# First batch by halves from a table of places; three batches load q once and sum their scores over two 32-row products

## The chip, the cores and the metric

The kernel runs on one NeuronCore of a Trainium2 chip. The metric is the device time of one execution in microseconds (us), median of several runs. PE is the matmul engine (TensorE), PEld its weight loads, DVE VectorE, ACT ScalarE, POOL GpSimd, SP the queue that issues most DMAs. Each engine runs its own instructions in the order in which the program writes them; semaphores tie the engines together.

## The reference

```python
# attention with 32 memory rows: B=8 batches, H=8 heads, S=576, D=64, M=32
a = exp(phi - max(phi, axis=2)); a /= a.sum(axis=2) + 1e-9
k_m, v_m = einsum('bhsm,bhsd->bhmd', a, k), einsum('bhsm,bhsd->bhmd', a, v)
scores = q @ k_m.T / sqrt(64);  attn = softmax(scores);  x = attn @ v_m      # 4608 tokens x 512
# first feed-forward: 512 -> 1536 -> 512
xn = x / sqrt(mean(x*x) + 1e-6) * rms_g
y = (silu(xn @ w_gate) * (xn @ w_val)) @ w_out
# second feed-forward: 512 -> 2048 -> 512
out = relu(y @ w_in)**2 @ w_out2
```

The five weight matrices come as float64, 8 bytes per number, and are turned into float32 on the core.

## The kernel before

**Main loop.** `phase_a` walks over items n = 0, 1, ... An item is one half batch (288 tokens) with one block f of 128 hidden columns: 6 matmuls for the gate (`g`), 6 for the value (`v`), and 12 (`y`) that multiply an earlier item's product with a block of w_out. A batch is 24 items (`NI`). Batch 0 alone takes its items in the order half 0 f 0-5, half 1 f 0-5, half 0 f 6-11, half 1 f 6-11, so that its later weights may come later. ACT takes the Silu of `g` (tile `sl`, L911), DVE multiplies with `v` (L915), ACT and POOL split the product in a high and a low part (`uh` L83, `ul` L92). `g` and `v` have one PSUM bank each, so the next item's gate matmuls wait until ACT has read `g`.

**Attention beside it.** The attention of batch b+1 is computed in steps (`p1`, `p3` to `p7` for the softmax of phi, `t1`, `a2` to `a6` for k_m and v_m, `a7` transposes q, `a8` the scores, `a9` to `a15` their softmax, `a18` to `a23` the mean square and its reciprocal root, `wp_mm` the product of v_m and the gate and value weights, `wp_hi` and `wp_lo` its split). `make_plan` puts each step at one of four places a to d of an item of batch b; `slot` runs them there, in program order, on every engine that the step uses. Batch 0 has no batch before it: `prologue` computes its attention, and also p1 to p6 of batch 1, before item 0.

**Conversions.** The weights are loaded raw by `raw_load` (512 KB each, five buffers) and converted by `conv_next`: two passes on ACT (L139, L140), one on DVE (L148), one on POOL (L152). In order they are the gate and value blocks 0 to 5 (four raws each) with the 12 blocks of w_out between them, 36 raws, then 32 raws of the second feed-forward. A finished gate and value block is 1 MB, goes to DRAM for the other batches (`w1d`, L630), and batch 0 takes it where it lies. `slot` puts three conversions in each of items 0 to 2, two in each of items 3 to 11, then one per item to item 17.

**Loads.** `load_q` brings one pair of heads and needs each row of q twice, at two column offsets (L250), since a 32 by 32 block transpose has to bring both halves of the 64 columns onto one set of 64 partitions: four DMAs of 144 KB per call, 16 per batch. All loads but k and v of batch 0 (ACT's queue) stand in SP's queue.

After the last item of batch 7 come the stages `phase_h` and `phase_z` of the second feed-forward, which the change doesn't touch.

Of the kernel before, what the change touches and what calls it, by code (L numbers as in the profile page):

```python
# [9 lines left out]
F32 = mybir.dt.float32  # L10
# [41 lines left out]
EPS = 1e-9  # L52
RMS_EPS = 1e-6
# [7 lines left out]

class Kernel:
# [41 lines left out]
    def raw_load(self, key):  # L111

        kind, f, cp = key
        nc = self.nc
        t = self.raw.tile([P, DM, 2], U32, tag="raw", bufs=5, name=f"raw_{kind}{f}_{cp}")
# [12 lines left out]
    def convert_start(self, key):  # L128

# [84 lines left out]
    def load_phi(self, b):  # L214
# [3 lines left out]
        for r in range(NR):  # L218
            hs = slice(4 * r, 4 * r + 4)
            nc.sync.dma_start(  # L220
                t[:, hs, 0 : 4 * M], src[r, :, 0:MAIN, :].rearrange("h (p j) m -> p h (j m)", j=4)
            )
            nc.sync.dma_start(t[0:TAIL, hs, 4 * M : 5 * M], src[r, :, MAIN:S, :].rearrange("h p m -> p h m"))
        self.st["ph", b] = t

    def load_kv(self, b, r):
        nc = self.nc
        dma = nc.sync if b else nc.scalar
        t = self.at.tile([P, 2, 4, 5 * D], F32, tag="kv", bufs=2, name=f"kv{b}_{r}")
        for i, src in enumerate((self.k, self.v)):  # L230
            src = src[b].rearrange("(j r) s d -> r j s d", r=NR)[r]
            dma.dma_start(t[:, i, :, 0 : 4 * D], src[:, 0:MAIN, :].rearrange("h (p j) d -> p h (j d)", j=4))
# [3 lines left out]
    def load_q(self, b, c):  # L236
        nc = self.nc

        if b == 0 and c == 2:
            t = self.at.tile([P, M + J * D], F32, tag="L", name="q0_2")  # L240
        elif b == 0 and c == 3:
            t = self.up.tile([P, M + J * D], F32, tag="st", name="q0_3")
        else:
            t = self.at.tile([P, M + J * D], F32, tag="q", bufs=2, name=f"q{b}_{c}")
        for hh in range(2):
            src = self.q[b, 2 * c + hh].rearrange("(p j) d -> p (j d)", j=J)
            for dh in range(2):
                p0 = (2 * hh + dh) * M
                c0 = M * (1 - dh)
                nc.sync.dma_start(t[p0 : p0 + M, c0 : c0 + J * D], src)  # L250
        self.st["q", b, c] = t

# [79 lines left out]
    def t1_first(self, b):  # L332

        t = self.att_ps(f"t1_{b}")
        ex = self.st["ph", b]
        for r in range(NR):
# [10 lines left out]
        self.st["t1"] = t  # L347
# [47 lines left out]
    def a5(self, b):  # L395
        t = self.att_ps(f"kvt_{b}")
        for i in range(2):
# [5 lines left out]
    def a6(self, b):  # L403
# [3 lines left out]
        nc.scalar.activation(kt, t[:, 0:P], AF.Copy)  # L407
# [10 lines left out]
    def a7(self, b, c):  # L418
        q = self.st.pop(("q", b, c))
        qt = self.at.tile([P, S], F32, tag="qt", bufs=4, name=f"qt{b}_{c}")  # L420
        self.nc.vector.transpose(
            qt.rearrange("p (j x) -> p j x", x=M),
            q[:, M : M + J * D].rearrange("p (j d) -> p j d", d=D)[:, :, 0:M],
        )
        self.st["qt", c] = qt

    def a8(self, b, hf):

        ts = [self.att_ps(f"sc_{b}_{hf}_{r}") for r in range(NR)]
        for j in range(4):  # L430
# [19 lines left out]
    def a10(self, b, r, engine="pool"):  # L450
        nc = self.nc
        x = self.st["L"][:, r, :].rearrange("p (j m) -> p j m", m=M)
        lm = self.st["lm"][:, r]
        nc.vector.tensor_reduce(lm, x, axis=AX.X, op=ALU.max)
        (nc.vector if engine == "dve" else nc.gpsimd).tensor_tensor(
            x, x, lm[:, :, None].to_broadcast([P, J, M]), op=ALU.subtract
        )

    def a12(self, b, r):
        x = self.st["L"][:, r]  # L460
        self.nc.scalar.activation(x, x, AF.Exp, scale=1.0 / D**0.5)

    def a13(self, b, r, engine="pool"):
        nc = self.nc
        x = self.st["L"][:, r].rearrange("p (j m) -> p j m", m=M)
        ls = self.at.tile([P, J], F32, tag="ls", bufs=2, name=f"ls{b}_{r}")
# [4 lines left out]
            x, x, ls[:, :, None].to_broadcast([P, J, M]), op=ALU.mult  # L471
        )

    def a15(self, b, r):
        if r == 0:
            self.st["an"] = []
        t = self.at.tile([P, S], F32, tag="qt", bufs=4, name=f"an{b}_{r}")
        self.nc.vector.transpose(t, self.st["L"][:, r, :])
        self.st["an"].append(t)

# [17 lines left out]
    def a19(self, b, hf, cp):  # L498
        at = self.at
        if hf == 0 and cp == 0:  # L500
            self.st["sq"] = [at.tile([P, S], F32, tag="qt", bufs=4, name=f"sq{b}_{i}") for i in range(2)]
            t = at.tile([P, NR, S], F32, tag="L", name=f"sqt{b}")
            self.st["sq"] += [t[:, 0], t[:, 1]]
        for t, sq in zip(self.st.pop("x"), self.st["sq"][2 * cp :]):
            self.nc.scalar.activation(sq[:, hf * HALF : (hf + 1) * HALF], t[:, 0:HALF], AF.Square)

    def sq_add(self, b, hf, engine="pool"):
        eng = self.nc.vector if engine == "dve" else self.nc.gpsimd
        hs = slice(hf * HALF, (hf + 1) * HALF)
        s = [x[:, hs] for x in self.st["sq"]]  # L510
# [3 lines left out]

    def sq_split(self, b, hf):
        t = self.wa.tile([P, NR, HALF], F32R, tag=("anh0", "anl0")[hf], name=f"sqs{b}_{hf}")
        self.split(t[:, 0], t[:, 1], self.st["sq"][0][:, hf * HALF : (hf + 1) * HALF], lo_engine="pool")
# [10 lines left out]
    def a20_first(self, b, hf):  # L528

        t = self.att_ps(f"ss{b}_{hf}")  # L530
        for i, sq in enumerate(self.st["sq"]):
            self.nc.tensor.matmul(
                t[:, 0:HALF], self.ones, sq[:, hf * HALF : (hf + 1) * HALF], start=(i == 0), stop=(i == 3)
            )
        self.st["ss", hf] = t[:, 0:HALF]

    def a21(self, b, hf, part=None):


        nc = self.nc  # L540
        y, a, t = (x[:, hf * HALF : (hf + 1) * HALF] for x in self.st["sq"][1:])
# [14 lines left out]
    def a23(self, b, hf):  # L556
        y = self.st.pop(("ry", hf))
# [18 lines left out]
    def wp_mm(self, b, ch):  # L576
# [12 lines left out]
        self.st["wp"] = ts  # L589
# [7 lines left out]
    def wp_hi(self, b, ch):  # L597
        hi = self.wa.tile([P, NR, DM], F32R, tag=f"wph{ch}", name=f"wph{b}_{ch}")
        for r, t in enumerate(self.st["wp"]):
# [3 lines left out]
    def wp_lo(self, b, ch):  # L603
        lo = self.wa.tile([P, NR, DM], F32R, tag=f"wpl{ch}", name=f"wpl{b}_{ch}")
        for r, t in enumerate(self.st.pop("wp")):
# [12 lines left out]
    def conv_end(self):  # L618
        if not self.started:
            return  # L620
        start = self.started.pop(0)
        kind, f, cp = start[0]
        if kind in "gv":
# [5 lines left out]
            if (kind, cp) == ("v", 1):  # L629
                self.nc.sync.dma_start(self.w1d[f], t.rearrange("p c n -> p (c n)"))  # L630
                self.st["w", 0, f] = t
        else:
# [4 lines left out]
            else:  # L637
                self.nc.sync.dma_start(self.w2d[kind, f], t)
        self.next_raw()

# [9 lines left out]


# [6 lines left out]
    def make_plan(self):  # L658
        self.early, self.warm_ps = 0, None
        self.w1, self.wo, self.wph, self.wpl, self.anh, self.anl = {}, {}, {}, {}, {}, {}  # L660
# [15 lines left out]

        self.plan = {}

        def at(n, pos, step, b, *args):
            if b < B:  # L680
                self.plan.setdefault((n, pos), []).append((step, (b, *args)))


        steps = [
            (1, "a", 0, "a7", 0),
            (1, "a", 0, "load_q", 2),
            (1, "d", 0, "t1"),
# [36 lines left out]
            (16, "c", 0, "sq_add", 0),
            (16, "c", 1, "p7"),
            (17, "b", 0, "a18", 1, 0),
            (17, "c", 0, "a19", 1, 0),
            (17, "d", 0, "a18", 1, 1),
            (17, "d", 0, "a19", 1, 1),
            (18, "a", 0, "sq_split", 0),  # L730
            (18, "c", 0, "sq_add", 1),
            (19, "b", 0, "a20", 0),
            (19, "c", 0, "a21", 0, 0),
            (20, "a", 0, "sq_split", 1),
            (20, "c", 0, "a21", 0, 1),
            (21, "a", 0, "a23", 0),
            (21, "b", 0, "a20", 1),
            (21, "b", 0, "an_split", 0),
            (21, "c", 0, "a21", 1, 0),
            (22, "c", 0, "a21", 1, 1),  # L740
            (23, "c", 0, "a23", 1),
            (24, "d", 0, "an_split", 1),
        ]
        for ch in range(NCH):
            i = 14 + 2 * ch
# [655 lines left out]
```

## Time and profile before

| | |
|---|---|
| median of 3 runs | 1568.76 us (1564.7 to 1569.13) |
| the profiled execution | 1563.32 us, its span 1561.5 us |
| busy in the span | PE 1504.9, DVE 1011.6, ACT 736.9, POOL 666.7 us |
| instructions | 29619 |

The span is the time from the first to the last instruction. An engine's busy time is the sum over its instructions; PE's weight loads run beside its matmuls and are counted apart. "PEclk" is the share of full clock that PE was granted.

### The profile page before, as it was taken

The numbers are of one execution on the slowest core, as the hardware profiler recorded it, in microseconds if no ns is written. First come the engines' busy times: TensorE is split into PE (matmuls) and PEld (weight loads), VectorE is DVE, ScalarE is ACT, GpSimd is POOL, SyncE is SP. The second block draws the span as 40 slices with busy tenths as digits, with TensorE's granted clock in tenths as the row PEclk, the third lists the DMA queues.
The fourth block names the chain that finished last, engine by engine and source line by source line (L and its number), as shares of the span: only waits on it lengthen the run. The fifth ranks groups of instructions, "written<-read, shape, count | busy, mean of one in ns | idle before, by whom it ended". The sixth has DMA issues, their size and how long they took to land. (4 is left out here: it accounts for less than half of the span.)

```text
span 1561.5 us, 29619 instructions
## 1 busy us (share of the span) xinstructions
PE 1504.9 (96%) x11594; PEld 1336.4 (86%) x11594; DVE 1011.6 (65%) x1543; ACT 736.9 (47%) x1318; POOL 666.7 (43%) x657
## 2 busy tenths in 40 slices
PE   6687999999999999999999999999999999999998
PEld 4465798998988889888899888888888999999998
DVE  5755654756456474653675867687667888777774
ACT  2666535445354553534455655566445333333332
POOL 0476634435344453523467521044003654444442
PEclk7788999999999999999999999999999999999999
DMA  9997674565836546432338774455648754444442
GB/s 262 282 310 284 234 203 174 171 169 190 237 137 211 179 160 190 145 99 97 110 139 315 245 263 155 147 162 200 241 170 260 226 147 136 136 125 141 132 132 68
DMA packets 206093, 288.22 MB, mean 185 GB/s; under 512 B 31520, under 2 KB 151328, under 8 KB 197888
## 3 DMA queue, kind: packets, MB, share of 16 engines
q1 hardware_dynamic: 201488, 276.36, 55.2%
q10 hardware_dynamic: 4400, 9.83, 1.8%
q8 instruction: 91, 1.49, 0.4%
q14 instruction: 50, 0.41, 0.1%
q0 software_dynamic: 64, 0.13, 0.0%
HBM read 197.27 MB, written 89.00 MB: 183 GB/s over the span
## 5 line engine op out<-in xcount | busy, mean ns | idle before, releaser
L92 POOL TENSOR_TENSOR ul<-sl,uh 128x288 fp32r<-128x288 f32 x192 | 167.9, 875 | 338.8 <-ACT uh L83 328.2
L881 PE MATMUL y<-uh,woh 128*128 128x288 f32 x768 | 232.5, 303 | 0.0
L882 PE MATMUL y<-uh,wol 128*128 128x288 f32 x768 | 227.6, 296 | 0.0
L883 PE MATMUL y<-ul,woh 128*128 128x288 f32 x768 | 226.8, 295 | 0.0
L83 ACT ACTIVATE S<-sr 128x1792 fp32r<-128x1792 f32 x72 | 122.6, 1703 | 194.7 <-PE z L1323 132.1
L915 DVE TENSOR_TENSOR sl<-sl,v 128x288 f32<-128x288 f32 x192 | 86.0, 448 | 198.3 <-PE v L867 140.8
L92 DVE TENSOR_TENSOR S<-sr,S 128x1792 fp32r<-128x1792 f32 x70 | 143.9, 2056 | 43.3 <-ACT S L83 43.3
L83 ACT ACTIVATE uh<-sl 128x288 fp32r<-128x288 f32 x192 | 85.2, 444 | 170.4 <-DVE sl L915 169.7
L881 PEld LDWEIGHTS y<-uh,woh 128*128 128x128 f32 x768 | 145.1, 189 | 16.0 <-issue 16.0
L882 PEld LDWEIGHTS y<-uh,wol 128*128 128x128 f32 x768 | 145.6, 190 | 0.0
L883 PEld LDWEIGHTS y<-ul,woh 128*128 128x128 f32 x768 | 145.2, 189 | 0.0
L1323 PE MATMUL z<-T,S 128*128 128x256 f32 x504 | 141.3, 280 | 2.1 <-DVE S L92 2.1
L1321 PE MATMUL z<-Wz,S 128*128 128x256 f32 x504 | 141.4, 281 | 0.0
L911 ACT ACTIVATE sl<-g 128x288 f32<-128x288 f32 x192 | 78.3, 408 | 133.4 <-PE g L867 128.0
L1323 PE MATMUL z<-Wz,S 128*128 128x256 f32 x504 | 141.3, 280 | 0.0
L1322 PE MATMUL z<-Wz,S 128*128 128x256 f32 x504 | 141.3, 280 | 0.0
L1321 PE MATMUL z<-T,S 128*128 128x256 f32 x504 | 141.2, 280 | 0.0
L1322 PE MATMUL z<-T,S 128*128 128x256 f32 x504 | 141.2, 280 | 0.0
L1210 ACT ACTIVATE c<-c 128x512 f32<-128x512 f32 (+1 forms) x120 | 70.1, 584 | 136.6 <-DVE c L1236 92.8
L1274 POOL TENSOR_TENSOR sr<-sr 128x256 f32<-128x256 f32 x72 | 98.1, 1363 | 81.8 <-DVE sr L1271 81.8
L865 PE MATMUL g<-anh,wph 128*128 128x288 f32 x384 | 118.4, 308 | 12.6 <-ACT sl L911 10.4
L865 PE MATMUL v<-anh,wph 128*128 128x288 f32 x384 | 119.7, 312 | 3.6 <-DVE sl L915 3.6
(202 smaller groups left out, 4306.4 us busy)
## 6 DMA issues: line engine op xcount, KB each, us to landing
w<-w SPq DMA_DIRECT2D x48, 1024.0 KB, 6.3
sr<-gd SPq DMA_DIRECT2D x144, 256.0 KB, 3.3
gd<-c SPq DMA_DIRECT2D x128, 256.0 KB, 3.0
q<-in_q_dram SPq DMA_DIRECT2D x128, 144.0 KB, 5.1
Wr<-wdi SPq DMA_DIRECT2D x6, 1792.0 KB, 8.9
y<-ys SPq DMA_DIRECT2D x16, 576.0 KB, 3.2
out_dram<-o SPq DMA_DIRECT2D x140, 64.0 KB, 1.7
raw_i<-in_moe_w_in_dram SPq DMA_DIRECT2D x16, 512.0 KB, 4.1
```

The lines of the kernel that those rows point to most:

```text
L83: nc.scalar.activation(hi, src, AF.Copy)
L92: f()
L865: nc.tensor.matmul(out, wh[:, r, cs], ah[:, r], start=(r == 0), stop=False)
L881: nc.tensor.matmul(y, hi[:, cs], uh, start=first, stop=False)
L882: nc.tensor.matmul(y, lo[:, cs], uh, start=False, stop=False)
L883: nc.tensor.matmul(y, hi[:, cs], ul, start=False, stop=last)
L911: nc.scalar.activation(sl, gp, AF.Silu)
L915: nc.vector.tensor_tensor(sl, sl, vp, op=ALU.mult)
L1274: nc.gpsimd.tensor_tensor(t[:, 7], t[:, 2], t[:, 5], op=ALU.subtract)
L1321: nc.tensor.matmul(out, sh, th, start=first, stop=False, **kw)
L1322: nc.tensor.matmul(out, sh, tl, start=False, stop=False, **kw)
L1323: nc.tensor.matmul(out, sl, th, start=False, stop=last, **kw)
```

## The change

`PLAN_0` and `PLAN` are tables of words "step.argument:place", a place being four times the item plus a to d as 0 to 3. `PLAN` holds nearly the places that the attention of batches 2 to 7 had before; `PLAN_0` holds those for batch 1's attention during batch 0, the second half of batch 0's own attention, and each conversion ("conv").

- Batch 0: the prologue takes half 0 (288 tokens) alone through scores, softmax and normalization; half 1 follows in items 0 to 3 (words that begin with 0). p1 to p6 of batch 1 move from the prologue and item 0 to items 2 to 4 (words that begin with 1). The mean square is summed per token into a column (`c20`), the reciprocal root is computed on 96 x 3 numbers (`c21`) and spread over the partitions by three matmuls (`c22`).
- q of batches 0 to 2 (`QS = 3`): `load_qs` brings four heads with one DMA, each row once. The scores are two accumulated products over 32 rows in place of one over 64, and the transpose of k_m goes from PE and ACT to DVE.
- Prologue loads: k on SP's queue, v on ACT's, phi's second half on ACT's; up to eight raws are asked for there (three in buffers that later hold weights). Stores of converted blocks are issued one conversion later. A first Exp and a first Silu on two numbers stand in the prologue; its idle matmuls (`warm`) go from 70 to 46.

```diff
+PLAN_0 = (
+    "0a8.1:0 conv.0:0 0a9.1:1 conv.1:1 conv.2:1 1load_q.0:2 1load_q.1:2 0a10.1:3 0a12.1:3 load_phi:3 "
+    "0a13.1:3 conv.3:4 conv.4:5 0a15.1:6 0wp_mm.1:6 0wp_hi.1:6 0wp_lo.1:6 conv.5:6 0a18.10:6 1load_kv.0:7 "
...
+    def load_qs(self, b, r, hf=None):
...
+        src = self.q[b].rearrange("(i r) (p j) d -> r i p (j d)", r=NR, j=J)[r]
+        nc.sync.dma_start(self.st["q", b, r][:, cs], src[:, :, cs])
...
     def a6(self, b):
...
-        nc.scalar.activation(kt, t[:, 0:P], AF.Copy)
+        if b < QS:
+            nc.vector.transpose(kt, self.st["kvz"][:, 0].rearrange("p r d -> p (r d)"))
+        else:
+            nc.scalar.activation(kt, t[:, 0:P], AF.Copy)
...
     def a8(self, b, hf):
...
+        if b < QS:
+            for r in range(NR):
+                for dh in range(2):
+                    for j in range(4):
+                        rs = slice(j * M, (j + 1) * M)
+                        self.nc.tensor.matmul(
+                            ts[r][rs, 0:HALF],
+                            self.st["kt"][rs, (2 * r + dh) * M : (2 * r + dh + 1) * M],
+                            self.st["qt", 2 * r + dh][rs, hf * HALF : (hf + 1) * HALF],
+                            start=dh == 0,
+                            stop=dh == 1,
+                        )
...
+    def c20(self, b, hf):
...
+        for c in range(NC):
+            cs = slice(c * CH, (c + 1) * CH)
+            for i, sq in enumerate(sqs):
+                self.nc.tensor.matmul(
+                    t[0:CH, 2 * c : 2 * c + 2], sq[:, cs], self.ones[:, 0:2], start=(i == 0), stop=(i == len(sqs) - 1)
+                )
...
     def prologue(self):
...
+        for c in range(KC):
+            self.a7s(0, c // 2, c % 2, 0)
+        h0 = ("h", 0)
+        self.a8(0, 0)
         self.conv_next()
+        self.a9(0, 0)
         self.conv_next()
...
+        self.conv_start()
+        self.a10(0, h0, "dve")
+        self.a12(0, h0)
+        nc.scalar.activation(self.at.tile([P, NR], F32, tag="mc", name="silu_first"), self.ones[:, 0:NR], AF.Silu)
+        self.conv_end()
+        self.a13(0, h0, "dve")
+        self.conv_end()
+        self.conv_start()
+        self.a15(0, h0)
...
+        self.c20(0, 0)
+        self.c21(0, 0)
+        self.c22(0, 0)
         self.wp_lo(0, 0)
         self.a23(0, 0)
         self.an_split(0, 0, "dve")
```

How the change moves instructions is seen at three places. SP's queue, from its start, before (`ph` is phi, `q_0` to `q_3` the four head pairs, `raw` a raw weight):

```order
L220 DMA ph_144<-in_phi_dram 128x4x128
L223 DMA ph_144<-in_phi_dram 64x4x32
L220 DMA ph_144<-in_phi_dram 128x4x128
L223 DMA ph_144<-in_phi_dram 64x4x32
L250 DMA q_0_159<-in_q_dram 32x1152 x4
L250 DMA q_1_164<-in_q_dram 32x1152 x4
L250 DMA q_2_169<-in_q_dram 32x1152 x4
L250 DMA q_3_174<-in_q_dram 32x1152 x4
L220 DMA ph_179<-in_phi_dram 128x4x128
```

and of the change:

```order
L243 DMA ph_145<-in_phi_dram 128x4x128
L244 DMA ph_145<-in_phi_dram 64x4x32
L253 DMA kv_0_150<-in_k_dram 128x4x256
L254 DMA kv_0_150<-in_k_dram 64x4x64
L253 DMA kv_1_155<-in_k_dram 128x4x256
L254 DMA kv_1_155<-in_k_dram 64x4x64
L287 DMA q_0_160<-in_q_dram 128x1x576
L287 DMA q_1_162<-in_q_dram 128x1x576
L836 DMA g_sb<-in_moe_rms_g_dram 128x4x1
L149 DMA raw_g_0_165<-in_moe_w_gate_dram 128x2x512
L149 DMA raw_g_1_167<-in_moe_w_gate_dram 128x2x512
```

Sixteen q loads became two for half 0 (two more follow after six raws), and the first raw moved ahead of them and of batch 1's phi, which stood before all raws. ACT in the prologue, from the softmax of the scores, before (`L` holds the scores, `cv` and `cr` the two passes of a conversion):

```order
L461 ACTIVATE L_390<-L_390 128x576 x2
L139 ACTIVATE cv_g_428<-raw_g_0_184 128x512
L140 ACTIVATE cr_g_429<-raw_g_0_184 128x512
L139 ACTIVATE cv_g_432<-raw_g_1_186 128x512
L140 ACTIVATE cr_g_433<-raw_g_1_186 128x512
L139 ACTIVATE cv_v_448<-raw_v_0_188 128x512
```

and of the change:

```order
L161 ACTIVATE cv_v_386<-raw_v_0_169 128x512
L162 ACTIVATE cr_v_387<-raw_v_0_169 128x512
L161 ACTIVATE cv_v_392<-raw_v_1_171 128x512
L162 ACTIVATE cr_v_393<-raw_v_1_171 128x512
L529 ACTIVATE L_382<-L_382 128x2x288
L870 ACT_TABLE_LOAD
L870 ACTIVATE silu_first<-ones 128x2
L161 ACTIVATE cv_g_411<-raw_g_0_173 128x512
```

Four conversions now stand ahead of the Exp of the scores, which stood ahead of all of them. ACT in items 0 and 1, before, from the first Silu:

```order
L911 ACTIVATE sl_603<-g_587 128x288
L139 ACTIVATE cv_v_612<-raw_v_0_454 128x512
L140 ACTIVATE cr_v_613<-raw_v_0_454 128x512
L83 ACTIVATE uh_621<-sl_603 128x288
L319 ACT_TABLE_LOAD
L319 ACTIVATE ph_179<-ph_179 128x8x128
L319 ACTIVATE ph_179<-ph_179 64x8x32
L139 ACTIVATE cv_v_627<-raw_v_1_469 128x512
L140 ACTIVATE cr_v_628<-raw_v_1_469 128x512
```

and of the change, from the split of item 0's product:

```order
L109 ACTIVATE uh_573<-sl_545 128x288
L529 ACT_TABLE_LOAD
L529 ACTIVATE L_382<-L_382 128x2x288
L161 ACTIVATE cv_o_600<-raw_o_0_430 128x512
L162 ACTIVATE cr_o_601<-raw_o_0_430 128x512
L947 ACT_TABLE_LOAD
```

The Exp of batch 1's phi has left this place (it stands in item 4), and the Exp of half 1's scores has come to it.

## Rows read from the trace of the kernel before

**Rows 1.** The page's 40 slices of the span: PE busy, granted clock, DMA.

```profile
PE   6687999999999999999999999999999999999998
PEclk7788999999999999999999999999999999999999
DMA  9997674565836546432338774455648754444442
```

**Rows 2.** Busy time in stretches: prologue, items 0-2, 3-5, 6-12, 13-23, batches 1, 2.

```profile
core 0: us, PE busy (x) PEld busy (x) DVE busy (x) ACT busy (x) POOL busy (x), PEclk, DMA share, GB/s
0.00:52.40 52.40, 35.67 (x341) 21.08 (x341) 30.12 (x59) 14.36 (x30) 5.98 (x11) 0.74 0.98 260
52.40:75.90 23.50, 14.74 (x224) 11.04 (x224) 16.83 (x28) 17.52 (x30) 12.15 (x10) 0.78 0.89 301
75.90:97.70 21.80, 16.50 (x108) 11.73 (x106) 11.72 (x20) 14.03 (x28) 17.25 (x16) 0.84 0.91 289
97.70:142.00 44.30, 33.56 (x235) 27.12 (x235) 22.09 (x38) 30.17 (x55) 30.78 (x26) 0.92 0.91 309
142.00:198.20 56.20, 51.85 (x385) 39.10 (x386) 39.32 (x67) 30.51 (x68) 34.40 (x34) 0.91 0.62 230
198.20:293.00 94.80, 94.44 (x833) 83.20 (x833) 55.24 (x101) 43.75 (x95) 42.36 (x46) 1.00 0.58 186
293.00:387.90 94.90, 94.57 (x835) 83.36 (x834) 54.45 (x98) 44.55 (x97) 42.42 (x47) 1.00 0.59 186
```

**Rows 3.** Who waited for whom, 30 to 160 us, longest in total first.

```profile
PE g L865 <- ACT sl L911: 10.4, 6, 3.2
...
ACT woh L83 <- POOL cv_o L152: 8.9, 4, 3.9
...
PE wp L582 <- DVE sqt L543: 8.0, 2, 7.7
...
ACT cv_o L139 <- DMA raw_o<-in_moe_w_out_dram: 3.6, 1, 3.6
```

**Rows 4.** Timeline of the prologue, one engine at a time: ACT, DVE, PE.

```profile
11.52 1.28 ACT L319 ACT_TABLE_LOAD   x1 [11.52 <-DMA kv<-in_v_dram]
...
11.22 0.27 DVE L313 TENSOR_TENSOR ph<-ph,mx 64x128 f32<-64x128 f32 x1
...
20.03 0.42 DVE L390 TENSOR_TENSOR kvz<-kv,rs 128x256 f32<-128x256 f32 x1 [0.26 <-PE kv L377]
...
24.96 0.78 DVE L421 STREAM_TRANSPOSE qt<-q 128x576 f32<-128x576 f32 x1 [1.85 <-DMA q<-in_q_dram]
...
28.73 0.71 DVE L454 TENSOR_REDUCE lm<-L 128x18 f32<-128x576 f32 x1
...
39.69 0.78 DVE L478 STREAM_TRANSPOSE an<-L 128x576 f32<-128x576 f32 x1
...
46.10 0.45 DVE L543 TENSOR_SCALAR sqt<-ss 128x288 f32<-128x288 f32 x1
...
49.82 0.46 DVE L553 SCALAR_TENSOR_TENSOR sq<-sqt,sq 128x288 f32<-128x288 f32 x1
...
42.24 2.29 PE L532 MATMUL ss<-sq,ones 128*128 128x288 f32 x4 [0.46 <-ACT sq L505]
...
52.37 0.40 PE L865 MATMUL g<-anh,wph 128*128 128x288 f32 x1 [2.00 <-ACT anh L83]
```

**Rows 5.** Timeline rows for single costs: small DVE operations, 40 small matmuls, one conversion.

```profile
15.33 0.17 DVE L364 RECIPROCAL rs<-rs 128x2 f32<-128x2 f32 x1
...
13.49 1.58 PE L340 MATMUL t<-ones,ph 128*32 128x2 f32 x80 [1.28 <-ACT ph L319]
...
60.62 0.66 ACT L140 ACTIVATE cr_v<-raw_v 128x512 int32<-128x512 uint32 x1
```

**Rows 6.** Timeline of PE: scores of one half of batch 1 (16 records, eight matmuls).

```profile
99.50 0.71 PE L433 MATMUL sc<-qt,kt 64*32 64x288 f32 x16
```

**Rows 7.** Timeline of SP's queue: the issue of batch 0's q.

```profile
3.42 17.83 SPq L250 DMA_DIRECT2D q<-in_q_dram  x16
```

More of the change, by code (lines that the diff above doesn't have):

```diff
@@ L114, in raw_load @@
         nc = self.nc
-        t = self.raw.tile([P, DM, 2], U32, tag="raw", bufs=5, name=f"raw_{kind}{f}_{cp}")
+        pool, tag, bufs = (self.wa, self.raw_more.pop(0), 1) if self.raw_more and len(self.raws) >= 5 else (self.raw, "raw", 5)
+        t = pool.tile([P, DM, 2], U32, tag=tag, bufs=bufs, name=f"raw_{kind}{f}_{cp}")
         src = {"g": self.w_gate, "v": self.w_val, "i": self.w_in2, "o": self.w_out1, "z": self.w_out2}[kind]
@@ L330, in p7, with t1_first @@
         nc.vector.tensor_tensor(es[0:TAIL, hs], es[0:TAIL, hs], ex[0:TAIL, hs, 4 * M : 5 * M], op=ALU.add)
-    def t1_first(self, b):
-        t = self.att_ps(f"t1_{b}")
+    def t1_first(self, b, r=None):
+        if not r:
+            self.st["t1"] = self.att_ps(f"t1_{b}")
+        t = self.st["t1"]
         ex = self.st["ph", b]
-        for r in range(NR):
+        for r in range(NR) if r is None else (r,):
             for jt in range(5):
@@ L396, in a5 @@
         t = self.att_ps(f"kvt_{b}")
-        for i in range(2):
+        for i in range(b < QS, 2):
             self.nc.tensor.transpose(
@@ L470, in a13, with a15 @@
         (nc.vector if engine == "dve" else nc.gpsimd).tensor_tensor(
-            x, x, ls[:, :, None].to_broadcast([P, J, M]), op=ALU.mult
+            x, x, ls[:, :, :, None].to_broadcast(list(x.shape)), op=ALU.mult
         )
[L474 to L479, printed above, removed]
+    def a15(self, b, part):
+        kind, i = part
+        if i == 0:
+            self.st["an"] = [None, None]
+        for r in (i,) if kind == "r" else range(NR):
+            if i == 0 or kind == "r":
+                pool, tag, bufs = (self.at, "qt", 4) if b else (self.wa, ("wph5", "wpl5")[r], 1)
+                self.st["an"][r] = pool.tile([P, S], F32, tag=tag, bufs=bufs, name=f"an{b}_{r}")
+            hs = slice(0, S) if kind == "r" else slice(i * HALF, (i + 1) * HALF)
+            self.nc.vector.transpose(self.st["an"][r][:, hs], self.st["L"][:, r, hs])
     def a18(self, b, hf, cp):
@@ L526, in a20 @@
         self.st["ss", hf] = t[:, 0:HALF]
[L528 to L535, printed above, removed]
     def a21(self, b, hf, part=None):
         nc = self.nc
-        y, a, t = (x[:, hf * HALF : (hf + 1) * HALF] for x in self.st["sq"][1:])
+        y, a, t = self.st["sq", hf][1:]
         if part != 1:
@@ L620, in conv_end @@
             return
-        start = self.started.pop(0)
+        start, n = self.started.pop(0), len(self.stores)
         kind, f, cp = start[0]
@@ L637, in conv_end @@
             else:
-                self.nc.sync.dma_start(self.w2d[kind, f], t)
+                self.stores.append((self.w2d[kind, f], t))
         self.next_raw()
+        old, self.stores = (self.stores, []) if not self.conv_keys else (self.stores[:n], self.stores[n:])
+        for to, t in old:
+            self.nc.sync.dma_start(to, t)
     def wo_split(self):
@@ L659, in make_plan @@
         self.early, self.warm_ps = 0, None
+        self.raw_more = ["wph3", "wpl3", "wpl4"]
+        self.stores = []
         self.w1, self.wo, self.wph, self.wpl, self.anh, self.anl = {}, {}, {}, {}, {}, {}
@@ L744, in make_plan @@
-        for ch in range(NCH):
-            i = 14 + 2 * ch
-            steps += [(i - 3, "d", 0, "wst_load", ch), (i, "a", 0, "wp_mm", ch), (i, "b", 0, "wp_ev", ch)]
-        at(1, "c", "a21", 0, 1, 0)
-        at(2, "a", "a23", 0, 1)
-        at(2, "d", "an_split", 0, 1)
-        for b in range(B - 1):
-            for i, pos, ahead, step, *args in steps:
-                if (b, step) == (0, "t1"):
-                    step = "t1_first"
-                at(NI * b + i, pos, step, b + 1 + ahead, *args)
@@ L756, in make_plan, with steps @@
-        at(0, "c", "p6", 1)
-        for n, ch in ((1, 1), (3, 2), (7, 3), (10, 4), (13, 5)):
-            at(n, "c", "wp_mm_early" if n == 1 else "wp_mm", 0, ch)
-            at(n, "c", "wp_hi", 0, ch)
-            at(n, "c" if n == 1 else "d", "wp_lo", 0, ch)
-        at(1, "c", "a21", 0, 1, 1)
+        def steps(text, b):
+            name, _, x = text.partition(".")
+            if name == "conv":
+                return [("conv_next", ())]
+            x = [int(c) for c in x]
+            if name[0].isdigit():
+                b, name = int(name[0]), name[1:]
+            elif name in ("p1", "p3", "p4", "p5", "p6", "p7", "load_phi", "load_kv") or name == "load_q" and x[0] < 2:
+                b += 1
+            if b < QS and name in ("load_q", "a7"):
+                if name == "load_q" and x[0] >= 2:
+                    return []
+                name, x = name + "s", x if name == "load_q" else [x[0] // 2, x[0] % 2]
+            if name in ("a10", "a12", "a13", "a15"):
+                x = [("r" if b else "h", x[0])]
+            if name in ("a10", "a13") and not b:
+                x.append("dve")
+            if name == "t1" and b == 1:
+                name = "t1_first"
+            if name == "wp_mm" and (b, x) == (0, [1]):
+                name = "wp_mm_early"
+            return [(n, (b, *x)) for n in (("a18", "a19") if name == "a18" else (name,)) if b < B]
@@ L764, in slot @@
+        self.plan = {}
+        for b in range(B - 1):
+            for word in (PLAN if b else PLAN_0).split():
+                text, _, q = word.partition(":")
+                self.plan.setdefault((NI * b + int(q) // 4, int(q) % 4), []).extend(steps(text, b + 1))
     def slot(self, n, pos):
-        for step, args in self.plan.get((n, pos), ()):
+        for step, args in self.plan.get((n, "abcd".index(pos)), ()):
             getattr(self, step)(*args)
@@ L785, in prologue @@
         nc = self.nc
-        nc.scalar.dma_start(self.g_sb, self.rms_g.rearrange("(c p) -> p c", p=P))
+        nc.scalar.activation(self.at.tile([P, NR], F32, tag="rs", name="exp_first"), self.ones[:, 0:NR], AF.Exp)
         self.load_phi(0)
@@ L789, in prologue @@
         self.load_kv(0, 1)
-        for c in range(KC):
-            self.load_q(0, c)
+        for r in range(NR):
+            self.load_qs(0, r, 0)
+        nc.sync.dma_start(self.g_sb, self.rms_g.rearrange("(c p) -> p c", p=P))
+        self.next_raw(6)
+        for r in range(NR):
+            self.load_qs(0, r, 1)
+        self.next_raw(8)
         self.load_phi(1)
-        self.next_raw()
         self.warm(30)
```

261 lines of the change are left out of this document (112 added, 149 removed), and 23 rows, old and new, of tables (PLAN, PLAN_0).

## The prediction

> **What bounds the kernel now.** I read the page's slices first: PE is at 9 tenths in all slices from the fifth on, and below that in the first four, about 156 us [rows 1]. So whatever can be won lies there, and everything that adds PE work later costs its full price. The stretches confirm it: batches 1 and 2 take 94.8 and 94.9 us with PE busy 94.4 and 94.6 of them, at a granted clock of 1.00 [rows 2]. Ahead of them lie a prologue of 52.4 us, in which no main matmul runs, and batch 0, which takes 23.5 + 21.8 + 44.3 + 56.2 = 145.8 us for the same 24 items, with five more weight products: 51 us more than a dense batch. That is what the change works on.
>
> What fills batch 0? PE is idle for 8.8 + 5.3 + 10.7 + 4.4 = 29 us of it and runs partly at the lower of its clock levels (mean 0.78 to 0.92, between half and full, which are 1.2 and 2.4 GHz) [rows 2]. PE's own waits there end with a Silu on ACT (10.4 us) and with the reciprocal root on DVE (7.7 in one piece) [rows 3]. ACT is busy 17.5 of 23.5 us in items 0 to 2, and a good deal of that is conversions, which stand in its order ahead of the next Silu. DMA is at 0.89 to 0.98 of its time until 142 us [rows 2], but a conversion waited for its raw only once, 3.6 us [rows 3]. So DMA is full yet mostly hidden; the chain of ACT, DVE and POOL in program order is what PE waits for.
>
> In the prologue the chain can be followed: a table load for the Exp from 11.52 to 12.80, the last q transpose waiting for its DMA until 24.96, softmax from 28.73 to the last transpose's end at 40.47, squares, their sum, the reciprocal root from 46.10 to 50.28, the first main matmul at 52.37 [rows 4].
>
> **The change, part by part.**
>
> *Prologue up to the softmax.* phi is ready for its Exp at 11.49, and the table load then stands in the way [rows 4]; the new first Exp loads the table beside the first DMAs, so 1.3 us go. SP needed 17.83 us to issue batch 0's sixteen q loads [rows 7]; now two DMAs carry half of the tokens and each row once, 0.59 MB in place of 2.36. k_m and v_m then set the time, not q. From them (about 18.7, that is the 20.03 at which their scaling began [rows 4], less 1.3) I count their scaling and transposes 1.3, four half transposes of q 4 x 0.41 (half of the 0.78 row) = 1.6, scores about 3.5 at the low clock, their transposes 0.5: softmax starts at 25.7, not 28.7: **-3.0**.
>
> *Softmax of one half.* One pass over 576 columns in place of two: half of the 11.74 from 28.73 to 40.47 [rows 4], 5.9. Both orders have conversion steps between them on DVE; the new one has one or two more per pass, 0.8, and its Exp stands behind four conversions on ACT, for which I add 1.0. 7.7 in place of 11.74: **-4.0**. This cover is thin: four conversions are 4 x 1.3 us of ACT [rows 5], and they need raws 0 to 3 landed by about 24 us. By bytes, 5.6 MB at 260 GB/s [rows 2] are there at 22.
>
> *Mean square.* Before, 42.24 (first sum) to 50.28 [rows 4]. Now 12 two-column matmuls; 40 others took 1.58 us [rows 5], these load three times as many columns of weights, so 0.5 to 2, I take 1.2; nine operations on 96 x 3 numbers at 0.17 (the smallest DVE row, [rows 5]) 1.5; three small matmuls 0.5; hand-overs 0.8. 4.0 in place of 8.0: **-4.0**. The second half's q transposes (1.6 on DVE) lie beside the squares; if q's second half, which stands behind six raws in SP's queue, lands after 34 us, they are late and the reciprocal root with them.
>
> First main matmul: 52.4 - 11.0 = about **41.4**.
>
> *Batch 0's items.* What left the prologue comes back here. Half 1 brings to ACT an Exp, four squares and one table load more: 576 and 4 x 288 columns at the pace of 0.66 for 512 [rows 5] and 1.28 [rows 4], 3.5. To DVE it brings a softmax pass of about 5 and score transposes of 0.9, less the 2.7 by which the root is shorter, and p1 to p5 of batch 1 two passes over 1024 columns, about 3 at the pace of 0.71 for 576 [rows 4]: 6.2. Part of it hides in engines that are 54 to 75% busy there [rows 2]; I take 5.0 as the loss in items 0 to 5 (bounds 3.5 and 9.7, the one engine alone and both in a row). Against it, the 7.7 us wait for the root (nine operations of half a batch behind conversions on DVE) becomes a wait for nine short ones, behind which the y matmuls and the next gate still stand in PE's order: I take 3.0 of it as won (0 to 5). In items 6 to 12, 44.3 us for seven items at 309 GB/s, 2.36 MB fewer have to be loaded by then (1.18 each for batches 0 and 1), 7.6 us of DMA time, of which the one seen wait is 3.6; I take 4.0 (0 to 8). In items 13 to 23 batch 2's 1.18 MB and the later conversions give 2.0 (0 to 5). Sum: 5 - 3 - 4 - 2 = **-4.0**.
>
> *Scores over 32 rows.* The eight matmuls of one half, over 64 rows each, took 0.71 us together [rows 6], so they ran at the same time. Now sixteen, of which four can run beside each other (row block j writes column block j) and the four groups follow each other; that is between one more group (0.7) and four times the row (2.8) for a half, I take 2.1, so +1.4. In batches 0 and 1 that lies where PE waits anyway; batch 2's two halves lie in the dense stretch: **+2.9**, less one transpose of k_m, 0.3. *Loads of q in fewer DMAs* free SP's queue, which is not waited for; the later stores of converted blocks and the 24 fewer idle matmuls, which run while PE waits, I cost at nothing: the first are read back half a batch later, the second only keep the clock up, and PE is not what the first items wait for.
>
> Sum: -11.0 - 4.0 + 2.6 = -12.4, and 1563.3 - 12.4 = 1550.9 for an execution like the profiled one. The runs shown lie 1.4 to 5.8 above that execution (median 5.4); I add 1.4 and forecast **1552 us**.
>
> **A shape that could turn the DMA saving around.** The new q load has four heads as the slowest dimension of its source, [4, 32, 576]; no load of the kernel before has fewer than 32 there. If a load is spread over no more DMA engines than that dimension has entries, q's 1.18 MB go through 4 engines of 16. At 309 GB/s and a share of 0.91 [rows 2] one engine moves 21 GB/s, so a batch's q keeps those four busy for 14.0 us, where the old double load kept all sixteen busy for 7.0, and every later load waits for its part on those four: +7 us of DMA time for each of three batches in place of -3.5.
> The Trainium skill (DMA: Bandwidth & Descriptors, the section on why a DMA increments its semaphore by 16) states such a rule: the number of engines is the largest up to 16 that divides the slowest dimension on both sides. No row here shows a load to which it would apply; by it the sum would be that of rival 2.
>
> **Rivals.**
> 1. *The loads were the true limit, and all of the saving is real*: DMA is at 0.9 until 142 us, which speaks for it; that raws were waited for once only speaks against it. The bounds of the items' terms then hold: 3.5 - 5 - 8 - 5 = -14.5 in place of -4, so about **1541**.
> 2. *q on four DMA engines*, as above. Two batches' q fall before 142 us, 14 us of DMA time; the slack there is a tenth of 90 us, so some 6 hide and 8 remain, and the 4.0 of items 6 to 12 turns to nothing as well, partly inside the same 8: 1552 + 8 = **1560**.
> 3. *The head start is given back*: batch 0 ends when its 36 conversions and their ACT, DVE and POOL steps are through (ACT and POOL 30 us in 44 in items 6 to 12 [rows 2]), whenever it began. Then 7 to 11 of the 11 us go: **1562 to 1566**, no change that can be measured.
> 4. *Slower: conversions block the Silu.* In the new order SP brings k, v, phi and q of batches 1 and 2 between the raws, and ACT's Silu stands behind the conversions. Fourteen conversions lie in items 2 to 8; if each waits 1 us or more for its raw, 14 us of PE waits eat the whole gain, from 17 us on the kernel is slower by over 0.3%; at 2 us each it is 12.4 - 28 = 15.6 worse, **1580**. Against it: eight raws are under way at the start, not five.
>
> **Chances and range.** The forecast 0.42 (its own range 1547 to 1557), rival 1 0.20, rival 2 0.20, rival 3 0.11, rival 4 0.07. About 0.3%, 4.7 us, is what a measurement of this kernel can tell from no change, so faster means below 1564. Faster: 0.42 + 0.20 + most of rival 2 (0.17) + 0.02 = 0.81; same 0.12; slower 0.07. The range takes in rivals 1 and 2 and the near end of rival 3: 1538 to 1565.
>
> **What the profile after would show.** First gate matmul at 39 to 44 us; Exp of phi with no table load before it; the root as nine DVE rows under 0.25 us. Item 6 at 85 to 92 (before 97.7), batch 1's first item at 181 to 186 (before 198.2), and batch 1's 24 items, which hold batch 2's scores, at about 97.4. ACT waiting on DMA for a raw after 45 us would speak for rivals 2 or 4; q's loads landing over 6 us apart for rival 2; a first matmul at 41 but batch 1 at 195 for rival 3. The prediction is wrong if half 0's chain waits for raws in the prologue, or if batches 3 to 7 are not the same as before.

## The result: slower, 1578.0 us in place of 1568.0

The changed kernel takes 1578.03 us (median of 4 runs, 1577.12 to 1579.29), the kernel before on the same chip 1567.97: a ratio of 1.0068 (95% interval 1.005 to 1.0086). The forecast was 1552 with a range to 1565. The profiled execution's span is 1575.5 us, 14.0 more than before.

Busy time in stretches of the changed kernel, with the edges of [rows 2] (prologue, items 0-1, 2-5, 6-12, 13-23, batches 1 and 2; the second edge lies an item earlier, at item 2):

```profile
0.00:48.60 48.60, 28.83 (x307) 18.35 (x307) 21.02 (x53) 14.10 (x27) 7.24 (x12) 0.65 0.85 249
48.60:69.50 20.90, 12.43 (x88) 6.47 (x88) 11.27 (x23) 15.95 (x30) 12.62 (x11) 0.74 0.54 185
69.50:98.60 29.10, 26.22 (x311) 23.40 (x309) 17.85 (x34) 19.96 (x38) 19.67 (x19) 0.83 0.95 301
98.60:143.60 45.00, 36.38 (x282) 30.00 (x282) 24.83 (x40) 23.83 (x50) 27.36 (x24) 0.89 0.98 290
143.60:207.80 64.20, 52.47 (x385) 40.61 (x386) 36.47 (x67) 38.23 (x76) 33.91 (x34) 0.87 0.64 230
207.80:305.40 97.60, 97.24 (x865) 84.64 (x864) 55.14 (x102) 43.61 (x94) 42.50 (x47) 1.00 0.53 168
305.40:400.30 94.90, 94.52 (x834) 83.33 (x833) 54.28 (x98) 44.55 (x97) 42.38 (x46) 1.00 0.59 186
```

The prologue is 3.8 us shorter than before [rows 2], not 11; items 0 to 12 take 95.0 us (before 89.6) and items 13 to 23 take 64.2 (before 56.2), so batch 1 begins at 207.8, 9.6 later than before. Batch 1 then costs 2.8 more, batch 2 nothing. In items 0 and 1 the DMA engines are busy for 0.54 of the time where they had been at 0.9, though loads were wanted. Finer stretches of the same kernel show it plainly, each with the share next to last:

```profile
40.00:50.00 10.00, 7.08 (x42) 6.40 (x35) 4.62 (x16) 2.91 (x6) 0.00 (x0) 0.50 0.98 369
50.00:60.00 10.00, 8.16 (x70) 4.17 (x68) 4.58 (x11) 7.38 (x14) 5.16 (x4) 0.90 0.35 120
60.00:70.00 10.00, 3.44 (x18) 1.66 (x19) 5.53 (x11) 7.68 (x16) 7.95 (x7) 0.61 0.70 241
```
```profile
53.00:60.00 7.00, 5.16 (x42) 2.75 (x34) 4.01 (x10) 4.38 (x8) 3.89 (x3) 1.00 0.25 97
157.00:159.00 2.00, 2.00 (x18) 0.83 (x4) 0.00 (x0) 1.97 (x4) 1.51 (x2) 0.50 0.26 104
```

The DMA share is the mean over 16 engines. From 53 to 60 us, behind batch 1's q, it stays at 0.25, which is four engines of sixteen; some time behind batch 2's q it is at that level again (0.26 from 157 to 159 us). SP's queue has the reason just ahead of the first stretch: batch 1's two loads of q, and behind them loads of phi of which one stood at issue for 9.15 us, where the two ahead of it took 1.2 and 2.2.

```profile
44.54 2.73 SPq L287 DMA_DIRECT2D q<-in_q_dram  x2
47.36 2.19 SPq L243 DMA_DIRECT2D ph<-in_phi_dram  x1
49.61 1.19 SPq L244 DMA_DIRECT2D ph<-in_phi_dram  x1
50.85 9.15 SPq L243 DMA_DIRECT2D ph<-in_phi_dram  x1
```

Batch 2's two loads of q are issued at 119.9 and 122.0. Twenty us later ACT waits for raws (first two rows), its Silu (third) stands behind those conversions, and PE's next gate (last row) waits 7 us for the Silu:

```profile
142.04 0.66 ACT L161 ACTIVATE cv_o<-raw_o 128x512 f32<-128x512 f32 x1 [6.90 <-DMA raw_o<-in_moe_w_out_dram]
...
149.88 0.66 ACT L161 ACTIVATE cv_o<-raw_o 128x512 f32<-128x512 f32 x1 [3.31 <-DMA raw_o<-in_moe_w_out_dram]
...
153.00 0.41 ACT L947 ACTIVATE sl<-g 128x288 f32<-128x288 f32 x1
...
153.46 0.61 PE L901 MATMUL g<-anh,wph 128*128 128x288 f32 x1 [6.98 <-ACT sl L947]
```

Before, the one wait for a raw in that part was 3.6 us [rows 3]; the forecast had named such waits after 45 us as the sign of rivals 2 and 4. From batch 2's first item (305.42, before 293.04) to the last item of batch 7 (856.32, before 842.35) another 1.6 us are lost. Of these 1.1 lie between the first and the last item of batch 7 (77.99 us, before 76.92), a stretch that the change doesn't touch and that takes from 76.9 to 81.7 us in the profiled executions of this text; batches 3 to 6 are each within 0.5 us of before.

In the prologue the last loads of k and v are late for PE (first two rows), the scores and the 24 records of `c20` run at the lower level (0.50, 1.2 GHz), and the root's nine operations take 0.16 us each, as forecast; the last row but one waits for them:

```profile
21.33 1.94 PE L414 MATMUL kv<-kv,ph 128*32 128x128 f32 x32 [4.53 <-DMA kv<-in_v_dram]
23.64 0.65 PE L414 MATMUL kv<-kv,ph 64*32 64x128 f32 x8 [0.38 <-DMA kv<-in_v_dram]
...
26.15 4.06 PE L485 MATMUL sc<-qt,kt 32*32 32x288 f32 x32 [0.84 <-DVE qt L472]
...
40.18 0.48 PE L596 MATMUL ss<-ones,sq_0h 128*96 128x2 f32 x2
...
46.08 1.57 PE L622 MATMUL rb<-ident,ryc 96*128 96x96 f32 x6 [1.90 <-DVE ryc L614]
48.67 0.61 PE L901 MATMUL g<-anh,wph 128*128 128x288 f32 x1 [1.02 <-ACT anh L109]
```

### The profile page after: what moved, and what is told of

Same layout as the page of the kernel before. It is cut to its first block, busy times and chain, and to the rows that moved or that the text cites. A ratio compares the mean times of both kernels' runs of the same rounds, so it can differ in the third digit from the quotient of the medians.

```text
span 1575.5 us, 29778 instructions
## 1 busy us (share of the span) xinstructions
PE 1512.3 (96%) x11707; PEld 1347.1 (86%) x11707; DVE 1000.9 (64%) x1552; ACT 741.4 (47%) x1321; POOL 661.8 (42%) x657
## 4 chain that ended last, share of the span: by engine, by line
PE 83%; DVE 5%; ACT 4%; DMA 4%; issue 2%; POOL 2%; SPq 0%; POOLq 0%; DVEq 0%; ACTq 0%
PE z L1357 7%; PE z L1359 7%; PE z L1358 7%; PE y L917 5%; PE y L919 5%; PE y L918 5%; PE h_S L1134 4%; PE h_S L1135 4%; PE h_S L1136 4%; PE v L901 3%; PE h_A L1134 3%; PE h_A L1135 3%; PE h_A L1136 3%; PE g L901 3%; PE v L902 3%; PE v L903 3%
## 5 line engine op out<-in xcount | busy, mean ns | idle before, releaser
L1310 POOL TENSOR_TENSOR sr<-sr 128x256 f32<-128x256 f32 x72 | 92.8, 1289 | 83.4 <-DVE sr L1307 83.4
```

## Experiments

Two questions: is it the shape of the q load (rival 2), and why does batch 0 not keep the head start? All are compared with the kernel before, which took 1566.9 to 1568.4 in these comparisons.

**1. The same load, one DMA per head** (32 source rows each, in all q loads of batches 0 to 2):

```diff
-        nc.sync.dma_start(self.st["q", b, r][:, cs], src[:, :, cs])
+        for i in range(4):
+            nc.sync.dma_start(self.st["q", b, r][i * M : (i + 1) * M, cs], src[i, :, cs])
```

> The changed kernel with its new q load cut into one DMA per head (32 rows each, the same bytes, four times as many DMAs). Theory 'few engines' (a q load whose source has four heads as its slowest dimension runs on a quarter of the DMA engines): the stretch in which the changed kernel had a DMA share of 0.54 (48.6 to 69.5 us) goes back to about 0.9, and the time falls from 1578 to 1555 to 1565 us. Theory 'order' (the loss comes from the new order of conversions and Silus on ACT, whatever the loads' shape): within 3 us of 1578.

Measured 1560.09, ratio 0.9965 (0.995 to 0.998): the same bytes in more DMAs are 18 us faster, and the change turns from a loss into a small gain. Its stretches (prologue, items 0-1, 2-5, 6-12, 13-23, batch 1):

```profile
0.00:41.20 41.20, 26.20 (x307) 16.40 (x307) 21.04 (x53) 14.00 (x27) 7.28 (x12) 0.80 0.86 248
41.20:62.20 21.00, 12.50 (x88) 6.54 (x88) 11.27 (x23) 15.87 (x30) 12.56 (x10) 0.74 1.02 319
62.20:91.00 28.80, 26.55 (x311) 23.72 (x309) 17.25 (x34) 19.86 (x38) 19.69 (x19) 0.83 0.88 271
91.00:134.50 43.50, 36.54 (x282) 30.30 (x283) 26.07 (x43) 27.27 (x54) 27.64 (x25) 0.88 1.01 316
134.50:191.30 56.80, 50.52 (x386) 39.11 (x385) 35.45 (x64) 34.75 (x72) 33.68 (x34) 0.91 0.67 248
191.30:288.90 97.60, 97.23 (x865) 84.63 (x864) 55.15 (x102) 43.58 (x94) 42.52 (x46) 1.00 0.53 168
```

The first main matmul is at 41.29, items 0 and 1 have a DMA share of 1.02 in place of 0.54, and no wait for a raw is left past the prologue. Items 13 to 23 are back at 56.8.

**2. Two heads per DMA** (slowest dimension 2):

```diff
+        for i in range(0, 4, 2):
+            nc.sync.dma_start(self.st["q", b, r][i * M : (i + 2) * M, cs], src[i : i + 2, :, cs])
```

> The changed kernel with its new q load cut into two DMAs of two heads each (the same bytes). 'Few engines': the slowest dimension is two now, each load takes twice as long as in the changed kernel, so 28 us per batch, and the time rises by 15 to 45 us. 'Order', or a cost that lies in the size of the loads: no change, within 3 us of 1578.

Measured 1603.97, ratio 1.0242 (1.0217 to 1.0266): more DMAs than in the change, and 26 us slower than it. The stretch that held 0.35 now holds 0.18, and in the middle of it the share stays at 0.13, two engines of sixteen:

```profile
60.00:70.00 10.00, 5.48 (x42) 3.34 (x39) 7.82 (x15) 6.00 (x9) 5.23 (x4) 0.84 0.18 67
70.00:80.00 10.00, 6.06 (x31) 4.25 (x30) 3.24 (x5) 7.01 (x15) 8.62 (x7) 0.50 0.23 75
62.00:71.00 9.00, 4.48 (x34) 1.99 (x33) 6.46 (x12) 7.00 (x11) 5.22 (x5) 0.82 0.13 50
```

With slowest dimensions of 2, 4 and 32, 1604, 1578 and 1560 us: neither bytes nor the number of DMAs sets the cost, the shape does. The rule of the Trainium skill (DMA: Bandwidth & Descriptors, the section on why a DMA increments its semaphore by 16) gives 2, 4 and 16 engines for them. The traces agree: 0.13 and 0.25 of sixteen engines are 2.1 and 4.0, and with 32 the share is 1.02; no view counts the engines of one DMA by itself.

**3. Loading once, undone** (`QS = 1`: batches 1 and 2 load q twice and score over 64 rows, as before), without and with the head-by-head load for what is left:

> The changed kernel with the new q load and the 32-row scores for batch 0 alone (QS = 1); batches 1 and 2 load q twice, as before. 'Few engines': two of the three slow loads are gone, 7 us of DMA time each, and the 2.8 us of longer scores in batch 1's items; 1561 to 1569 us. 'Order': 2.8 us less alone, about 1575 us.

> Both edits: QS = 1, and batch 0's q with one DMA per head. 'Few engines': below QS = 1 alone by the one remaining slow load, 1555 to 1562 us; against the first kernel of this set it shows whether loading q of batches 1 and 2 once is worth its 2.8 us of scores (if DMA binds, up to 7 us slower than the first; if not, up to 3 us faster). 'Order': about 1575 us.

Measured 1564.82 (ratio 0.9982, 0.9967 to 0.9998) and 1559.44 (0.995, 0.9935 to 0.9965). With the first, the first main matmul stays late (48.47) but batch 1 starts at 197.15 in place of 207.80; with the second they are at 41.78 and 191.76. Batch 0's own four loads so cost 5.4 us, those of batches 1 and 2 the rest, some 13 (experiment 4 has 4.0 and 13.9). Against experiment 1 the second starts batch 1 at the same time (191.76 and 191.30) with 2.36 MB more to load, though without batch 1's 32-row scores in batch 0. So fewer bytes are worth no more there than those scores cost, some 3 us by the row at the end of this text, and not 7.6; and batch 1's items are 2.7 us shorter (94.9) without batch 2's.

**4. Only the loads of batches 1 and 2 as in the change**, batch 0's by head:

```diff
+        if b:
+            nc.sync.dma_start(self.st["q", b, r][:, cs], src[:, :, cs])
+        for i in () if b else range(4):
```

> The changed kernel with batch 0's four q loads (two halves of two rows) made head by head, and those of batches 1 and 2 left as one DMA of four heads each. All by head took 1560.1 us, all in one DMA 1578.0; first main matmul at 41.29 and 48.67, batch 1's first item at 191.30 and 207.80. Theory 'few engines, everywhere' (each DMA of four heads holds back the loads behind it by its own length): first main matmul at 41 to 42, items 0 to 12 within 3 us of the run by head, and the loss of about 10 us comes in items 13 to 23, where batch 2's q is loaded: 1568 to 1572. Theory 'prologue' (only the loads at the start matter, for later ones are hidden): 1559 to 1562. Theory 'head start given back' (batch 0 ends when the slowest load and conversion are through, so a loss at the start is no loss at the end): 1576 to 1579.

Measured 1574.02 (7 runs, 1568.47 to 1577.47), ratio 1.0036 (1.0017 to 1.0054). The first theory (1568 to 1572) and the third (1576 to 1579) both miss by 2 us, 'prologue' (1559 to 1562) by 12. 'Prologue' falls. The place is nearly that of the first: items 13 to 23 take 67.4 us, 10.6 more than by head. But item 13 begins at 140.0 (134.5 by head, where the theory allowed 3 us) and the first main matmul at 43.9. Of these last 2.6 us 1.5 are there when k_m is transposed (19.30 against 17.84), where the two kernels have run the same program: so much do executions differ in the prologue.

In the profiled execution the lead over the change shrinks from 4.8 us at the first main matmul to 3.6 at item 13, 2.0 at item 15 and 0.4 at batch 1 (207.4): ACT waits 10.2 us for `raw_o` between 120 and 166 us, as in the change, and PE 8.5 us for the Silu. That is the third theory's picture, but this execution was the slowest of the seven (1577.47), and the median lies 4.0 below the change's. How much of a lead at the start reaches the end is therefore not shown.

**5. The first items in another order.** With the loads mended, 150.0 us of batch 0's items are still 8 above the forecast's 141.8 and 4 above before. PE's waits from 41 to 191 us in experiment 1 have changed their kind: the Silu (10.4 before [rows 3]) has 1.5 left and the root is nearly gone, but half 1's products now make PE wait:

```profile
PE x L561 <- DVE an L552: 4.0, 1, 4.0
PE x L561 <- ACT sq L581: 3.9, 1, 3.9
PE sc L486 <- DVE wpl L712: 3.9, 1, 3.9
PE x L561 <- DVE wpl L712: 3.5, 1, 3.5
PE mx_None L333 <- DVE wpl L712: 2.3, 1, 2.3
PE rb L623 <- DVE ryc L615: 1.9, 1, 1.9
PE g L902 <- ACT sl L948: 1.5, 3, 0.8
```

On top of the second kernel of experiment 3 the words of `PLAN_0` were moved, and nothing else; then also batch 1's scores:

```diff
-0a13.1:3 conv.3:4 conv.4:5 0a15.1:6 0wp_mm.1:6 0wp_hi.1:6 0wp_lo.1:6 conv.5:6 0a18.10:6 ... 0a18.11:7 ... 0c20.1:9
+0a13.1:3 conv.3:4 0wp_mm.1:5 0wp_hi.1:5 conv.4:5 0wp_lo.1:6 0a15.1:6 conv.5:6 0a18.10:7 ... 0a18.11:9 ... 0c20.1:11
...
-a8.0:31 a9.0:32 ... a8.1:32 a9.1:34 ... p3:35 ... p4:44 ... p5:45
+a8.0:35 a9.0:36 ... a8.1:37 a9.1:38 ... p3:36 ... p4:46 ... p5:47
```

> The kernel with q loaded head by head and 32-row scores for batch 0 alone (1559.4 us, span 1555.1), with the steps of half 1 placed otherwise in items 1 to 3: the second chunk's weight product and its conversion to two parts one place earlier (ahead of a conversion on ACT), the two products of half 1 (x) one and two places later, so that the second stands behind item 2's gate, and its mean square two places later. No work is added or left out. There item 2's gate began at 62.70, behind waits of 4.0 and 3.9 us for x, while the second chunk's low part could be ready near 57. Theory 'order' (the head start of 11 us was lost because PE, in program order, waits in items 1 and 2 for half 1's softmax and squares): those two waits go, item 2's gate starts at 56 to 59, and 3 to 6 us of it reach batch 1's first item (now 191.8) and the end: 1553 to 1557. Theory 'conversions' (batch 0 ends when its 36 conversions are through, however it began): item 2 begins earlier, but batch 1's first item stays within 1 us of 191.8 and the time at 1558 to 1561. Theory 'work' (the PE time of half 1, 9.4 us, was moved out of the prologue and is what fills the items): no wait is worth much, 1557 to 1560.

> The same, and in items 7 to 11 batch 1's scores placed one item later (behind item 8's gate, value and output products instead of ahead of them) and its largest-value product half an item later. There PE waited 4.3 us at 103.7 and 2.3 us for the low part of a weight product (on DVE), since the scores' PSUM banks are those of that product. Theory 'order': both waits go, item 13 starts 5 to 7 us earlier than in the run with the first items alone and at least 4 of it reach batch 1: 1549 to 1553. Theory 'conversions': item 13 moves by under 2 us and the time stays within 2 us of that run. Theory 'work': as 'conversions' to within 2 us.

Measured 1555.65 (0.9921, 0.9907 to 0.9935) and 1555.39 (0.9925, 0.9912 to 0.9939). The first has the numbers of 'order': item 2's gate at 58.63 in place of 62.70, batch 1 at 188.33 in place of 191.76, the time 3.8 less. 'Work' (1557 to 1560) misses, and 'conversions' falls for these items: most of what is won in item 2 is there 130 us later. Yet of the two waits only the one for the squares went; the other grew from 4.0 to 5.3:

```profile
PE x L561 <- DVE an L552: 5.3, 1, 5.3
```

The second is a miss of 'order': one of its two waits went, the other shrank from 2.3 to 1.6, and others came (3.0 us for score transposes, 5.7 in all for the Silu in place of 3.1, and 4.7 us on ACT for a raw in place of 0.7). Item 13 began 1.4 us earlier (128.68), batch 1 at 188.94, and nothing is won: for this edit 'conversions' and 'work' had it right.

**6. Half 1's products behind item 2's gate, the second chunk's split earlier still**, and the same with batch 1's q loaded once (`QS = 2`):

```diff
-0a13.1:3 conv.3:4 0wp_mm.1:5 0wp_hi.1:5 conv.4:5 0wp_lo.1:6 ... 0a18.10:7 ... 0a18.11:9 ... 0c20.1:11 ... 0c22.1:12
+0a13.1:3 0wp_mm.1:4 0wp_hi.1:4 0wp_lo.1:4 conv.3:4 conv.4:5 ... 0a18.10:9 ... 0a18.11:11 ... 0c20.1:12 ... 0c22.1:13
```

> The run with the first items placed otherwise, and more of it: the second chunk's conversion to two parts straight behind half 1's Exp on ACT (there it stood behind one conversion, a table load and the Silu), and both products of half 1 (x) behind item 2's gate and value products. In that run PE waited 5.3 us for x's operand ahead of item 2's gate at 58.63 and the low part of the second chunk was ready at 56.7. Theory 'order': item 2's gate starts at 55 to 57, and what is won (2 to 3.5 us) is still there at batch 1 (now 188.33): 1552 to 1554. Theory 'conversions' (batch 0 ends when its conversions are through): batch 1 stays at 188 to 189, 1555 to 1556.

> As the run with x behind item 2's gate, and batch 1's q too loaded once (head by head) with its scores as two sums over 32 rows: 1.18 MB less to load in batch 0, and some 3 us more of PE time for the scores in items 7 to 9. Theory 'order' (PE and the chain of its operands set the time in batch 0): 1 to 3 us slower than that run. Theory 'DMA' (the loads set the time until about 142 us): 2 to 4 us faster than it.

Measured 1559.14 (0.9949, 0.993 to 0.9968) and 1561.26 (0.9956, 0.9941 to 0.9971). Both theories missed the first: item 2's gate came at 57.29, little earlier, and then the squares that free the banks for the second product stood on ACT behind three conversions and a Silu (timeline of ACT from the last of the three, then PE):

```profile
65.99 0.65 ACT L161 ACTIVATE cv_v<-raw_v 128x512 f32<-128x512 f32 x1
66.84 0.67 ACT L162 ACTIVATE cr_v<-raw_v 128x512 int32<-128x512 uint32 x1 [0.20 <-POOL w L174]
67.42 0.40 ACT L948 ACTIVATE sl<-g 128x288 f32<-128x288 f32 x1
67.71 0.71 ACT L581 ACTIVATE sq<-x 128x288 f32<-128x288 f32 x2
...
68.17 1.52 PE L561 MATMUL x<-an,kvz 32*64 32x288 f32 x8 [5.11 <-ACT sq L581]
```

Batch 1 started 9.0 later than in the first kernel of experiment 5 (197.34). The profiled execution was the slowest of its six (1563.28); by the medians the loss is 3.5 us. It is the direction that 'order' gives for a new wait of 5.1 us ahead of item 3's gate; the placing was worse. Between the two kernels of this pair the intervals overlap, so the last pair of theories stays undecided.

## Why the prediction was wrong, step by step

**The step that failed first: "q on four DMA engines ... some 6 hide and 8 remain".** The mechanism was named and given 0.20; its price was 18 us (1578 against 1560), not 8, so the forecast stood on the wrong case and rival 2's own time was as wrong. Two errors are in the price. It counted two batches' q, those of batches 0 and 1, while batch 2's is issued before 142 us too (119.9 and 122.0); and it put batch 0's at no time in the prologue, where the first main matmul came 7.4 us later (48.67 against 41.29). Nearly all of that was lost ahead of the scores, for k_m was late, in the change (first row) against experiment 1 (second):

```profile
24.82 0.31 DVE L445 STREAM_TRANSPOSE kt<-kvz 128x128 f32<-128x128 f32 x1
```
```profile
17.84 0.31 DVE L446 STREAM_TRANSPOSE kt<-kvz 128x128 f32<-128x128 f32 x1
```

And it took the DMA engines' average slack as cover (a tenth of 90 us, that is 9, of which it let 6 hide). Here four loaded engines were not covered by idle time of the other twelve (share 0.25 from 53 to 60 us): raws queued behind landed late, the conversion that waited stood ahead of a Silu on ACT, and PE stopped. That is rival 4's chain, set off by rival 2's cause. I had priced them apart.

**Prologue, -11.0 to 41.4: the total right where the load doesn't interfere** (41.29 in experiment 1), **in part by luck.** There the softmax began at 24.0 (forecast 25.7) and took 7.5 us (forecast 7.7). The mean square, with the three matmuls behind the root, took 5.7 us (34.60 to 40.27; forecast 4.0). The one error pays for the other. `c20`'s twelve matmuls were mis-sized: forecast 1.2 us, 2.2 at full clock in experiment 1 (first row) and 4.0 at the lower level in the changed kernel (second). The three matmuls took 1.57 us, forecast 0.5.

```profile
34.60:36.80 2.20, 2.20 (x32) 2.11 (x24) 0.00 (x0) 1.09 (x2) 0.00 (x0) 0.99 1.11 357
```
```profile
40.10:44.10 4.00, 4.00 (x32) 3.91 (x24) 0.00 (x0) 1.08 (x2) 0.00 (x0) 0.50 0.99 376
```

**Batch 0's items, -4.0: wrong by 8 even with the loads mended** (150.0 against 141.8). The term costed half 1's work on ACT and DVE, never on PE. PE is busy 126 us in experiment 1's items (the sum of its four rows) and 117 before [rows 2]. That the prologue's PE time fell by the same 9.5 us (35.7 to 26.2) is chance, for 3.3 of it are the idle matmuls left out (before, then experiment 1):

```profile
L782 PE MATMUL warm<-ones 128*128 128x256 bf16 x70 | 13.1, 372 | 1.4 <-DVE ones L172 1.4
```
```profile
L827 PE MATMUL warm<-ones 128*128 128x256 bf16 x46 | 9.7, 401 | 1.4 <-DVE ones L194 1.4
```

By line, the items' products for x take 7.0 us in place of 3.2, the scores 8.9 in place of 1.4 (half 1's, and batch 1's over 32 rows), and half 1's mean square and its spread 3.7; the weight products take 13.9 in place of 21.4. In items 0 to 5, 2.5 us more were lost than forecast, and experiment 5's first kernel, set beside the kernel it was made from (49.7), gives 2.1 back by placing alone (47.5, forecast 47.3). In items 6 to 12 that kernel comes near the forecast 40.3 (40.9), but with half of the bytes that the forecast wanted saved (batch 1's) still loaded, so its reason isn't borne out. Items 13 to 23 stay at 56 to 60 in place of 54.2 in every kernel with mended loads. They take 56.4 and 56.8 us where batch 1's q is loaded once (`QS` 2 and 3) and 58.2 to 60.3 where it is loaded twice, and of these kernels only the latter let ACT wait for a raw past the prologue (0.7 to 4.7 us in all). The first kernel of experiment 3, which reaches item 13 late (142.3) and loads it twice, takes 54.8. So the loads may set the time there; no run separates it.

**32-row scores: right.** Batch 1 took 97.6 for 97.4. PE's records by line over that batch have 4.3 us for its scores, where two halves took 1.4 [rows 6]:

```profile
L485 PE MATMUL sc<-qt,kt 32*32 32x288 f32 x64 | 4.3, 404 | 0.0
```

**Rival 1** (all DMA saving real, 1541) falls with experiments 1 and 3. **Rival 3** (head start given back) holds in part: of 11.1 us at the first main matmul of experiment 1, 6.9 are left at batch 1. Some 3 of what was lost came back by another order alone (experiment 5); the rest is PE's added work and what happens in items 13 to 23, which is argued and not shown.

## What to carry to other kernels

Look at the slowest dimension of a load's source before its bytes: here the same bytes cost 18 us more with 4 there than with 32. The greater number of DMAs did cost SP time (11.0 us for the first eight q loads, 1.4 for two), and yet the first main matmul came 7.4 us earlier. When a price rests on slack of an engine group, follow what stands in order behind the late transfer (conversion, Silu, gate) and add that stop. When work moves from a prologue into a busy stage, charge it to the engine that is the bound there, and place its products behind work that is ready, but see what their operands then stand behind on other engines: in experiment 6 that cost more than the place won.

## What the hardware showed unexpectedly

A DMA share that stood at 0.25 or 0.13 meant a full queue on a few engines, not an idle one: SP stood 9.15 us at one issue while 97 GB/s moved. The fastest versions made, the two of experiment 5 (1555.6 and 1555.4 us, not to be told apart), have the head-by-head load for batch 0, q loaded twice afterwards, and a changed order of steps in items 1 to 3 (the second in items 7 to 11 too).
